# Sink keys once in K, and q's low half over all 128 rows

## The chip, the cores and the metric

One core of one Trainium2 chip. The metric is the device time of the program in microseconds (us), the median of several runs. A profiled execution is read beside it.

## The reference

Three layers in a row, all in float32. First attention with a window and sinks: 4 batches, 8 heads, 768 positions, head width 64. A position sees itself and the 127 before it, and the first 4 positions (the sinks) always.

```python
scores = scale * np.matmul(q, k.transpose(0, 1, 3, 2))
is_sink = pos[None, :] < int(n_sink)
in_window = (rel >= 0) & (rel < int(window))
scores = np.where(is_sink | in_window, scores, -1000000000.0)
a = np.exp(scores - np.max(scores, axis=-1, keepdims=True))
out = np.matmul(a / (np.sum(a, axis=-1, keepdims=True) + 1e-09), v)
```

The result, 3072 tokens of 512, goes through a dense layer, `g = h - tanh(h)` with `h = x @ w_in` (width 2048) and `g @ w_out`. Then each token is sent to one of 8 experts (width 1024, relu) by the largest of 8 logits, and the expert's output is weighted by the token's gate.

## The kernel before

The tokens are worked on in 12 chunks of 256. A chunk's attention is 8 units, one a head; a unit U is two query blocks t = 0, 1 of 128 positions. Each chunk then passes the dense layer in 16 steps of 128 hidden columns (`L1`, `gact`, `L2`), and `r_route` gives its tokens their places in the experts' pages. After the last chunk the pages of 256 tokens pass their experts (`m_L1`, `m_L2`).

float32 products are made from float32r operands split into a high half (a cast) and a low half (the value minus the cast): three products, high by high, high by low, low by high. For the scores of units from 14 on (`nf=14`; the first 14 take plain float32) the halves are stacked in the 128 rows, since the head width is 64. `a_split` (line 292) gets q and k with their 64 rows twice. ScalarE casts q to A over 128 rows (299). POOL overwrites A's rows 64 to 127 with q's low half (300, recorded at the helper's line 216). Two DMAs on the SP queue fill B with A's halves the other way round (301, 302). VectorE casts k to K (303) and overwrites K's lower rows with k's low half (304). `a_S` (307) multiplies A and then B by the same 288 columns of K (314, 315), into one PSUM tile s.

K's 448 columns are: the block before, 32 sink keys, block 0, the 32 sink keys again, block 1. Query block t takes the 288 columns from 160 t on: the block before it, the sinks, its own block. Own and earlier scores are merged by a predicated copy on VectorE (319), where the mask `mgt` is set for columns beyond the row, so that 128 columns hold the window. Then VectorE adds the mask and takes the row's extreme (326), ScalarE takes the exponential (328), POOL normalises (337), TensorE transposes (347, 348), POOL selects the two triangles (355), and TensorE multiplies by V (413 to 419), which ScalarE casts and POOL subtracts just as A is (288, 289; rows 128). In the dense layer POOL makes the low half of g with the same kind of subtraction (201, line 216 too), on 128 rows.

`r_route` ends, once a chunk, with two indirect DMAs on POOL's own queue that scatter the tokens' gates and numbers to their slots in DRAM (656). They come up on POOL between the subtractions.

The order: `run_chunks` gives every action a due time (unit U at 2 U - 15.64 steps, chunk c at 16 c, with offsets from the table of options in line 45), sorts by it, and emits. The framework then lays out each engine's queue by a simulated timeline of its own, so neighbours can change places (line 302's copy is issued ahead of line 301's), and puts in the semaphore waits. Each engine runs its own queue in order. Loads of q, k, v wait on the SP queue for one of two buffers (`raw=2`), A, B and K have two each (`sp=2`), V one. SP also issues the copies to B and the weights' loads.

Of the kernel before, what the change touches and what calls it, by code (L numbers as in the profile page):

```python
# [11 lines left out]
U8 = mybir.dt.uint8  # L12
AF = mybir.ActivationFunctionType
ALU = mybir.AluOpType
PSUM = bass.MemoryType.PSUM

P = 128
B, H, S, D = 4, 8, 768, 64
# [2 lines left out]
NCH = NT // CH  # L21
NF = DFF // P
SK = 32
KW = 2 * (P + SK) + P
QW = P + SK + P
NEG = -8.0e9
NE, FF = 8, 1024
# [9 lines left out]
def f32(ap):  # L37
    return ap.bitcast(F32)


class Kern:
# [9 lines left out]
    def consts(self, cp):  # L51
        nc = self.nc
        self.ident = cp.tile([P, P], F32, name="ident")
        make_identity(nc, self.ident)
        self.mgt = cp.tile([P, P], U8, name="mgt")
        nc.vector.memset(self.mgt, 1)
        nc.gpsimd.affine_select(out=self.mgt.bitcast(mybir.dt.int8), in_=self.mgt.bitcast(mybir.dt.int8),
                                pattern=[[1, P]], base=0, channel_multiplier=-1,
                                compare_op=ALU.is_gt, fill=0.0)

    def scalars(self, cp):

# [188 lines left out]
    def a_load(self, U):  # L251
# [3 lines left out]
        if U < self.o["nf"]:  # L255
            if U % 2:
                q = f32(self.spp.tile([P, CH], F32R, tag="A", name=f"q{U}"))
                k = f32(self.spp.tile([P, KW], F32R, tag="K", name=f"k{U}"))
            else:
                q = self.rawp.tile([P, CH], F32, tag="q", name=f"q{U}")  # L260
                k = self.rawp.tile([P, KW], F32, tag="k", name=f"k{U}")
            nc.sync.dma_start(q[:D], self.a["q"][b, h, j, :D])
# [4 lines left out]
        q = p.tile([P, CH], F32, tag="q", name=f"q{U}")  # L267
        k = p.tile([P, KW], F32, tag="k", name=f"k{U}")
        nc.sync.dma_start(q, self.a["q"][b, h, j])
# [22 lines left out]
    def a_split(self, U):  # L292
        nc = self.nc
        u, p = self.u[U], self.spp
        q, k = u.pop("q"), u.pop("k")
        A = p.tile([P, CH], F32R, tag="A", name=f"A{U}")
        Bt = p.tile([P, CH], F32R, tag="B", name=f"B{U}")
        K = p.tile([P, KW], F32R, tag="K", name=f"K{U}")
        self.cast(self.e("qhi", U < 16), A, q)
        self.sub(self.e("qlo", U < 16), A[D:], q[D:], f32(A[D:]))  # L300
        nc.sync.dma_start(f32(Bt[:D]), f32(A[D:]))
        nc.sync.dma_start(f32(Bt[D:]), f32(A[:D]))
        self.cast(self.e("khi", U < 16), K, k)
        self.sub(self.e("klo", U < 16), K[D:], k[D:], f32(K[D:]))
        u.update(A=A, B=Bt, K=K)

    def a_S(self, U, t):
        nc = self.nc
        u = self.u[U]
        i = 2 * ((U // H) % 3) + t  # L310
        s = self.ps("s", F32, f"s{U}_{t}")
        kt = u["K" if "K" in u else "k"][:, t * (P + SK):t * (P + SK) + QW]
        if "A" in u:
            nc.tensor.matmul(s[:, :QW], u["A"][:, t * P:(t + 1) * P], kt, start=True, stop=False)
            nc.tensor.matmul(s[:, :QW], u["B"][:, t * P:(t + 1) * P], kt, start=False, stop=True)
        else:
            nc.tensor.matmul(s[:, :QW], u["q"][:D, t * P:(t + 1) * P], kt[:D], start=True, stop=True)
        if i > 0:
            nc.vector.copy_predicated(s[:, P + SK:QW], self.mgt, s[:, :P])
        p = self.smp  # L320
        if t == 0:
            u["sm"] = p.tile([P, 2], F32, tag="sm", name=f"sm{U}")
            u["e"] = {}
        nm = p.tile([P, 1], F32, tag="nm", name=f"nm{U}_{t}")
        e = p.tile([P, SK + P], F32, tag="e", name=f"e{U}_{t}", bufs=self.o["be"])
        nc.vector.tensor_tensor_reduce(out=e, in0=s[:, P:QW], in1=self.mask[min(i, 2)], scale=-0.125,  # L326
                                       scalar=3.0e38, op0=ALU.add, op1=ALU.min, accum_out=nm)
        nc.scalar.activation(e, e, AF.Exp, bias=nm, scale=-1.0, accum_out=u["sm"][:, t:t + 1])  # L328
        u["e"][t] = e
        if t == 1:  # L330
            nc.gpsimd.tensor_scalar(out=u["sm"], in0=u["sm"], scalar1=1e-9, scalar2=1.0, op0=ALU.add, op1=ALU.mult)
            nc.vector.reciprocal(u["sm"], u["sm"])  # L332
# [92 lines left out]
    def general(self):  # L425
        tc, nc = self.tc, self.nc
        SH = S // 2
        with ExitStack() as st:
# [7 lines left out]
            for i in range(S // P):  # L436
# [6 lines left out]
                k = kp.tile([P, S], BF16, name=f"gkeep{i}")  # L443
                nc.vector.tensor_tensor(out=k, in0=inw, in1=sink, op=ALU.max)
                keep.append(k)
            for b in range(B):
                for h in range(H):
                    n = f"{b}_{h}"
                    q = lp.tile([D, S], F32, tag="q", name="gq" + n)
                    k = lp.tile([D, S], F32, tag="k", name="gkk" + n)  # L450
                    v = lp.tile([P, S // P, D], F32, tag="v", name="gv" + n)
                    for j in range(S // CH):
                        nc.sync.dma_start(q[:, j * CH:(j + 1) * CH], self.a["q"][b, h, j, :D])
                        for r in range(2):
                            o = P + SK + r * (P + SK)
                            nc.sync.dma_start(k[:, (2 * j + r) * P:(2 * j + r + 1) * P], self.a["k"][b, h, j, :D, o:o + P])
                        nc.sync.dma_start(v[:, 2 * j:2 * j + 2], self.a["v"][b, h, j, :, 1:3])
                    for i in range(S // P):
                        m = f"{n}_{i}"
                        s = wp.tile([P, S], F32, tag="s", name="gs" + m)  # L460
                        for z in range(2):
                            ps = pp.tile([P, 512], F32, tag="s", name=f"gps{m}_{z}")
                            nc.tensor.matmul(ps[:, :SH], q[:, i * P:(i + 1) * P], k[:, z * SH:(z + 1) * SH],
                                             start=True, stop=True)
                            nc.scalar.mul(s[:, z * SH:(z + 1) * SH], ps[:, :SH], 0.125)
                        t = wp.tile([P, S], F32, tag="t", name="gt" + m)
                        nc.vector.tensor_mul(s, s, keep[i])
                        nc.vector.tensor_scalar(out=t, in0=keep[i], scalar1=1.0e9, scalar2=-1.0e9, op0=ALU.mult, op1=ALU.add)
                        nc.vector.tensor_add(s, s, t)
                        nm = wp.tile([P, 1], F32, tag="nm", name="gnm" + m)  # L470
                        sm = wp.tile([P, 1], F32, tag="sm", name="gsm" + m)
                        nc.vector.tensor_reduce(out=nm, in_=s, axis=mybir.AxisListType.X, op=ALU.max, negate=True)
                        nc.scalar.activation(s, s, AF.Exp, bias=nm, accum_out=sm)
                        nc.vector.tensor_scalar(out=sm, in0=sm, scalar1=1e-9, scalar2=None, op0=ALU.add)
                        nc.vector.reciprocal(sm, sm)
                        nc.vector.tensor_scalar(out=s, in0=s, scalar1=sm, scalar2=None, op0=ALU.mult)
                        x = pp.tile([P, 512], F32, tag="x", name="gx" + m)
                        for z in range(S // P):
                            tp = pp.tile([P, 512], F32, tag="t", name=f"gtp{m}_{z}")
                            nc.tensor.transpose(tp[:, :P], s[:, z * P:(z + 1) * P], self.ident)  # L480
                            at = wp.tile([P, P], F32, tag="at", name=f"gat{m}_{z}")
                            nc.scalar.copy(at, tp[:, :P])
                            nc.tensor.matmul(x[:D, :P], v[:, z], at, start=(z == 0), stop=(z == S // P - 1))
                        xo = wp.tile([D, P], F32, tag="xo", name="gxo" + m)
                        nc.vector.tensor_copy(xo, x[:D, :P])
                        c = b * (S // CH) + i // 2
                        o = (h % 2) * D
                        nc.sync.dma_start(self.xd[c, h // 2, o:o + D, (i % 2) * P:(i % 2 + 1) * P], xo)
# [459 lines left out]
def layouts(inp):  # L948
    import numpy as np
    a = {}  # L950
    q, k, v = inp["q"], inp["k"], inp["v"]
# [3 lines left out]
    sk = kT[..., :SK]  # L955
    blk = [kT[..., i * P:(i + 1) * P] for i in range(6)]
    hs = []
    for j in range(3):
        b0 = 2 * j
        one = np.concatenate([blk[max(b0 - 1, 0)], sk, blk[b0], sk, blk[b0 + 1]], axis=3)  # L960
        hs.append(np.concatenate([one, one], axis=2))
    a["k"] = np.ascontiguousarray(np.stack(hs, axis=2))
    vb = [v[:, :, i * P:(i + 1) * P] for i in range(6)]
# [3 lines left out]
    for j in range(3):  # L967
        b0 = 2 * j
# [35 lines left out]
```

## Time and profile before

| | us |
|---|---|
| median of 3 runs (1222.67 to 1223.86) | 1222.8 |
| the profiled execution | 1225.8 |
| its span, first to last instruction | 1224.0 |
| TensorE matmuls busy | 1135.9 (93%) |
| VectorE busy | 885.5 (72%) |
| ScalarE busy | 757.4 (62%) |
| POOL busy | 657.7 (54%) |
| mean granted TensorE clock, share of 2.4 GHz | 0.96 |

The engines' names in the profile are PE (TensorE; PEld its weight loads), DVE (VectorE), ACT (ScalarE), POOL (GpSimd) and SPq (the SP queue, which only issues DMAs). Attention and the dense layer take the first 850 us or so, the experts the rest. An engine's idle time costs something only where TensorE, the busiest, waits for it in the end. Tiles carry the program's names, with buffer numbers left out.

### The profile page before, as it was taken

How to read it: one execution, taken by the hardware profiler on the slowest of the kernel's cores; microseconds unless marked ns; L12 is line 12 of the kernel's file. 1: busy time of each engine (PE TensorE's matmuls, PEld its weight loads, DVE VectorE, ACT ScalarE, POOL GpSimd, SP SyncE). 2: the span in 40 equal slices, each digit the busy share in tenths (PEclk: the TensorE clock that was granted, in tenths of full speed). 3: DMA queues.
4: the chain of work that ended last, by engine and by line, in shares of the span. 5: the costliest groups of instructions: out<-in, count | busy, mean ns of one | idle time of the engine just before them, and what ended most of it. 6: DMA issues, size and time to landing. Idle time of an engine off the chain costs nothing. (4 is left out here: it accounts for less than half of the span.)

```text
span 1224.0 us, 23714 instructions
## 1 busy us (share of the span) xinstructions
PE 1135.9 (93%) x7171; PEld 994.8 (81%) x7171; DVE 885.5 (72%) x2419; ACT 757.4 (62%) x2123; POOL 657.7 (54%) x973
## 2 busy tenths in 40 slices
PE   7879998999899899999899999999798999999993
PEld 3447787988789789989789988988687989999992
DVE  6889896888778687978778887966647566666720
ACT  3445765777577678767577877775726555555620
POOL 4987865777667668767667767763302211211200
PEclk9859998999999899999999999999998999999997
DMA  7654232333323233333333323200909777777500
GB/s 206 203 187 137 75 91 62 102 80 102 60 76 90 71 88 85 98 69 104 60 91 83 104 66 87 81 12 19 343 19 327 238 226 213 222 241 219 168 26 6
DMA packets 88256, 147.98 MB, mean 121 GB/s; under 512 B 18864, under 2 KB 64432, under 8 KB 88112
## 3 DMA queue, kind: packets, MB, share of 16 engines
q1 hardware_dynamic: 83184, 133.16, 37.2%
q0 software_dynamic: 4928, 13.14, 3.0%
q8 instruction: 61, 1.00, 0.4%
q14 instruction: 83, 0.68, 0.2%
HBM read 122.86 MB, written 13.17 MB: 111 GB/s over the span
## 5 line engine op out<-in xcount | busy, mean ns | idle before, releaser
L172 PE MATMUL h<-xt,wi 128*128 128x256 f32 x2304 | 356.1, 290 | 9.9 <-DVE gz L188 9.0
L246 PE MATMUL acc<-wo,g 128*128 128x512 f32 x1152 | 334.5, 407 | 24.0 <-POOL g L216 23.1
L172 PEld LDWEIGHTS h<-xt,wi 128*128 128x128 f32 x2304 | 320.5, 194 | 40.4 <-DVE gz L188 12.4
L246 PEld LDWEIGHTS acc<-wo,g 128*128 128x128 f32 x1152 | 198.6, 192 | 53.1 <-POOL g L216 26.0
L216 POOL TENSOR_TENSOR g<-gz,g 128x256 fp32r<-128x256 f32 x192 | 153.4, 802 | 82.3 <-ACT g L211 78.4
L735 DVE TENSOR_TENSOR ml<-mr,mh 128x1024 fp32r<-128x1024 f32 x104 | 127.9, 1236 | 53.4 <-ACT mh L734 51.8
L778 PE MATMUL mh<-mxt,mh 128*128 128x256 f32 x832 | 157.9, 286 | 3.2 <-DVE mxt L768 2.5
L795 PE MATMUL macc<-mh,mg 128*128 128x512 f32 x416 | 147.9, 401 | 4.3 <-DVE mg L782 4.3
L778 PEld LDWEIGHTS mh<-mxt,mh 128*128 128x128 f32 x832 | 138.1, 193 | 12.1 <-DVE mxt L768 2.9
L189 ACT ACTIVATE u<-u,kt 128x256 f32<-128x256 f32 x192 | 97.8, 509 | 80.2 <-DVE gz L188 73.8
L355 POOL TENSOR_SCALAR_AFFINE_SELECT X<-fl 128x512 fp32r<-128x512 f32 (+1 forms) x192 | 119.2, 643 | 33.6 <-DVE fl L385 24.5
L804 POOL DMA_INDIRECT out_dram<-mo,mi x26 | 28.5, 1096 | 200.2 <-ACT mo L803 196.0
L734 ACT CAST mh<-mr 128x1024 fp32r<-128x1024 f32 x104 | 108.6, 1052 | 40.9 <-PE macc L795 25.2
L188 DVE TENSOR_TENSOR gz<-u,h 128x256 f32<-128x256 f32 x192 | 78.9, 414 | 57.5 <-POOL g L216 34.2
L778 PE MATMUL mh<-mxt,ml 128*128 128x256 f32 x416 | 118.5, 286 | 0.0
L194 DVE SCALAR_TENSOR_TENSOR gz<-gy,gz 128x256 f32<-128x256 f32 x192 | 108.3, 570 | 9.2 <-ACT gy L185 2.7
L328 ACT ACTIVATE e<-e,nm 128x160 f32<-128x160 f32 x192 | 82.0, 427 | 48.0 <-DVE nm L326 46.5
L211 ACT CAST g<-gz 128x256 fp32r<-128x256 f32 x192 | 77.0, 402 | 44.4 <-DVE gz L194 29.7
L337 POOL TENSOR_SCALAR e<-e,sm 128x160 f32<-128x160 f32 x192 | 96.9, 515 | 11.6 <-DVE sm L332 9.6
L216 POOL TENSOR_TENSOR A<-q,A 64x256 fp32r<-64x256 f32 x82 | 69.4, 846 | 56.3 <-issue 14.0
L781 ACT ACTIVATE mg<-mh 128x256 fp32r<-128x256 f32 x104 | 40.3, 387 | 94.2 <-PE mh L778 88.3
L185 ACT ACTIVATE gy<-u,k 128x256 f32<-128x256 f32 x192 | 96.5, 510 | 2.5
(211 smaller groups left out, 2270.5 us busy)
## 6 DMA issues: line engine op xcount, KB each, us to landing
mr<-in_moe_w_dram SPq DMA_DIRECT2D x104, 512.0 KB, 4.7
k<-in_k_dram SPq DMA_DIRECT2D x82, 224.0 KB, 2.7
v<-in_v_dram SPq DMA_DIRECT2D x96, 128.0 KB, 2.3
q<-in_q_dram SPq DMA_DIRECT2D x82, 128.0 KB, 2.2
B<-A SPq DMA_DIRECT2D x164, 64.0 KB, 2.1
rawi<-in_moe_w_in_dram SPq DMA_DIRECT2D x16, 512.0 KB, 5.7
rawo<-in_moe_w_out_dram SPq DMA_DIRECT2D x16, 512.0 KB, 5.6
x2d<-x SPq DMA_DIRECT2D x24, 256.0 KB, 2.2
```

The source lines that it names most:

```text
L172: nc.tensor.matmul(h[:, :CH], w[:, wl, k * P:(k + 1) * P], x[:, xl, k], start=(n == 0), stop=(n == 11))
L185: nc.scalar.activation(y, u, AF.Square, bias=self.k0, scale=K1)
L189: nc.scalar.activation(u, u, AF.Relu, bias=self.kt, accum_out=self.over[:, n:n + 1])
L194: nc.vector.scalar_tensor_tensor(out=z, in0=y, scalar=KC, in1=z, op0=ALU.add, op1=ALU.mult)
L216: (self.nc.vector if eng == "v" else self.nc.gpsimd).tensor_tensor(out=out, in0=a, in1=b, op=ALU.subtract)
L246: nc.tensor.matmul(o, g[:, gl, t * P:(t + 1) * P], w[:, wl], start=(f == 0 and n == 0), stop=(f == NF - 1 and n == 2))
L337: self.nc.gpsimd.tensor_scalar(out=e, in0=e, scalar1=r, scalar2=1.0, op0=ALU.mult, op1=ALU.mult)
L355: self.nc.gpsimd.affine_select(out=out, in_=in_, pattern=[[0, n], [s, P]], base=0, channel_multiplier=-s, compare_op=ALU.is_gt if prev els ...
L734: nc.scalar.copy(hi, r)
L735: nc.vector.tensor_sub(lo, r, f32(hi))
L778: nc.tensor.matmul(h, w[:, k * P:(k + 1) * P], x[:, xl, k], start=(n == 0), stop=(n == 11))
L795: nc.tensor.matmul(self.macc[g][t], gt[:, gl, t * P:(t + 1) * P], w[:, DM:], start=(f == 0 and n == 0), stop=(f == n8 - 1 and n == 2))
```

## The change

K keeps the sink keys once, in 416 columns: the block before, the sinks, block 0, block 1. Query block 0 takes columns 0 to 287 as before. Block 1 takes columns 128 to 415, which are the sinks, block 0, block 1; its own scores are copied over those of its neighbour where a second mask, `mge`, is set (row not less than column), and the 160 columns from the front are used. B is no longer filled by two DMAs from A: A stays q's high half in all 128 rows, and POOL writes q's low half to all 128 rows of B in one subtraction. With K's high half above and its low half below, A and B times K give the same four products as before.

```diff
-KW = 2 * (P + SK) + P
+KW = 3 * P + SK
...
-        nc.gpsimd.affine_select(out=self.mgt.bitcast(mybir.dt.int8), in_=self.mgt.bitcast(mybir.dt.int8),
-                                pattern=[[1, P]], base=0, channel_multiplier=-1,
-                                compare_op=ALU.is_gt, fill=0.0)
+        self.mge = cp.tile([P, P], U8, name="mge")
+        nc.vector.memset(self.mge, 1)
+        for m, s, op in ((self.mgt, 1, ALU.is_gt), (self.mge, -1, ALU.is_ge)):
+            m = m.bitcast(mybir.dt.int8)
+            nc.gpsimd.affine_select(out=m, in_=m, pattern=[[s, P]], base=0, channel_multiplier=-s,
+                                    compare_op=op, fill=0.0)
...
         self.cast(self.e("qhi", U < 16), A, q)
-        self.sub(self.e("qlo", U < 16), A[D:], q[D:], f32(A[D:]))
-        nc.sync.dma_start(f32(Bt[:D]), f32(A[D:]))
-        nc.sync.dma_start(f32(Bt[D:]), f32(A[:D]))
+        self.sub(self.e("qlo", U < 16), Bt, q, f32(A))
...
-        kt = u["K" if "K" in u else "k"][:, t * (P + SK):t * (P + SK) + QW]
+        kt = u["K" if "K" in u else "k"][:, t * P:t * P + QW]
...
-        if i > 0:
+
+        if t:
+            nc.vector.copy_predicated(s[:, SK:P + SK], self.mge, s[:, P + SK:QW])
+        elif i > 0:
             nc.vector.copy_predicated(s[:, P + SK:QW], self.mgt, s[:, :P])
+        s = s[:, :P + SK] if t else s[:, P:QW]
...
-        nc.vector.tensor_tensor_reduce(out=e, in0=s[:, P:QW], in1=self.mask[min(i, 2)], scale=-0.125,
+        nc.vector.tensor_tensor_reduce(out=e, in0=s, in1=self.mask[min(i, 2)], scale=-0.125,
...
-        one = np.concatenate([blk[max(b0 - 1, 0)], sk, blk[b0], sk, blk[b0 + 1]], axis=3)
+        one = np.concatenate([blk[max(b0 - 1, 0)], sk, blk[b0], blk[b0 + 1]], axis=3)
```

`general`, which runs only where the inputs don't fit the fast path, takes its columns of k from the new places.

## Rows read from the trace of the kernel before

**Rows 1.** The page, part 1: busy time, share of the span, instructions.

```profile
PE 1135.9 (93%) x7171; PEld 994.8 (81%) x7171; DVE 885.5 (72%) x2419; ACT 757.4 (62%) x2123; POOL 657.7 (54%) x973
```

**Rows 2.** Stretches: length, busy (instructions) of PE, PEld, DVE, ACT, POOL, PEclk, DMA share, GB/s.

```profile
395.83:468.56 72.73, 67.45 (x448) 61.35 (x447) 54.13 (x171) 49.76 (x162) 47.42 (x77) 0.95 0.33 81
468.56:529.31 60.75, 60.47 (x423) 55.67 (x422) 52.10 (x170) 46.42 (x153) 46.56 (x74) 1.00 0.32 87
...
667.20:728.01 60.81, 60.50 (x423) 55.70 (x422) 52.09 (x170) 46.43 (x153) 46.63 (x74) 1.00 0.32 87
```

**Rows 3.** TensorE's waits from 190 to 802 us: total us, times, longest.

```profile
PE acc L246 <- POOL g L216: 22.4, 8, 5.6
PE R L413 <- POOL V L216: 4.6, 2, 2.3
PE T L347 <- POOL e L337: 1.5, 5, 0.5
```

**Rows 4.** TensorE in order of time: start, us, what [idle before, releaser].

```profile
266.02 1.19 PE L246 MATMUL acc<-wo,g 128*128 128x512 f32 x4 [0.75 <-POOL g L216]
...
405.96 1.22 PE L246 MATMUL acc<-wo,g 128*128 128x512 f32 x2 [4.51 <-POOL g L216]
```

**Rows 5.** POOL in order of time around 400 us.

```profile
395.83 0.97 POOL L656 DMA_INDIRECT xs<-pl,sl  x1 [0.30 <-issue]
396.82 0.75 POOL L216 TENSOR_TENSOR g<-gz,g 128x256 fp32r<-128x256 f32 x1
403.70 0.72 POOL L216 TENSOR_TENSOR A<-q,A 64x256 fp32r<-64x256 f32 x1 [6.13 <-issue]
```

**Rows 6.** DMA issues from 395.7 to 396.6 us: KB, us to landing.

```profile
k<-in_k_dram SPq DMA_DIRECT2D x1, 224.0 KB, 6.2
xs<-pl,sl POOLq DMA_INDIRECT x1, 7.6
```

**Rows 7.** POOL in order of time around 470 us.

```profile
468.56 0.97 POOL L656 DMA_INDIRECT xs<-pl,sl  x1 [0.30 <-DMA B<-A]
...
470.29 0.74 POOL L216 TENSOR_TENSOR V<-v,V 128x256 fp32r<-128x256 f32 x1
...
475.50 0.74 POOL L216 TENSOR_TENSOR A<-q,A 64x256 fp32r<-64x256 f32 x1
```

**Rows 8.** Groups by line and form: busy us, mean ns | idle before, releasers.

```profile
L216 POOL TENSOR_TENSOR A<-q,A 64x256 fp32r<-64x256 f32 x82 | 69.4, 846 | 56.3 <-issue 14.0 <-DMA k<-in_k_dram 12.2 <-ACT A L211 9.2
L216 DVE TENSOR_TENSOR K<-k,K 64x448 fp32r<-64x448 f32 x82 | 68.1, 830 | 2.6
L216 POOL TENSOR_TENSOR V<-v,V 128x256 fp32r<-128x256 f32 x82 | 62.9, 767 | 29.5 <-ACT V L211 25.2 <-PE T L348 1.9 <-DMA B<-A 0.2
...
L213 DVE CAST K<-k 128x448 fp32r<-128x448 f32 x82 | 43.8, 534 | 0.0
```

**Rows 9.** ScalarE in order of time: the cast for the g behind V.

```profile
399.37 0.39 ACT L211 CAST g<-gz 128x256 fp32r<-128x256 f32 x1
```

**Rows 10.** Stretches right behind stalls, columns as in rows 2.

```profile
201.75:207.00 5.25, 5.25 (x19) 4.86 (x20) 3.92 (x10) 3.23 (x11) 4.56 (x9) 0.50 0.16 49
...
736.50:739.50 3.00, 3.00 (x12) 2.81 (x13) 2.42 (x8) 1.59 (x6) 2.90 (x6) 0.51 0.28 78
801.13:805.00 3.87, 3.87 (x25) 3.50 (x26) 2.94 (x9) 2.50 (x9) 3.17 (x7) 1.00 0.14 38
```

**Rows 11.** The page, part 6: DMA issues, KB each, us to landing.

```profile
k<-in_k_dram SPq DMA_DIRECT2D x82, 224.0 KB, 2.7
...
B<-A SPq DMA_DIRECT2D x164, 64.0 KB, 2.1
```

**Rows 12.** The SP queue's own waits: total us, times, longest.

```profile
SPq L302 <- PE s L315: 213.8, 71, 5.3
```

**Rows 13.** TensorE in order of time: the unit whose A was made at 403.70.

```profile
416.01 0.30 PE L314 MATMUL s<-K,A 128*128 128x288 f32 x1
```

**Rows 14.** The start: POOL in order of time.

```profile
9.62 0.19 POOL L331 TENSOR_SCALAR sm<-sm 128x2 f32<-128x2 f32 x1 [5.49 <-ACT e L328]
```

More of the change, by code (lines that the diff above doesn't have):

```diff
@@ L454, in general @@
                         for r in range(2):
-                            o = P + SK + r * (P + SK)
+                            o = P + SK + r * P
                             nc.sync.dma_start(k[:, (2 * j + r) * P:(2 * j + r + 1) * P], self.a["k"][b, h, j, :D, o:o + P])
```

## The prediction, made before the changed kernel was run

> **What bounds the kernel now.** Read the page first: TensorE is busy for 93% of the span [rows 1], so time can only be won where it waits or where its clock is low. Then the stretches by chunk: from one chunk's last scatter of slots (line 656) to the next. The stretch from 468.56 us has TensorE at work for 60.47 of 60.75 us at full clock; the one before it takes 72.73 us with 67.45 us of work at a mean clock of 0.95 [rows 2]. Both hold a chunk's work (448 matmuls against 423). So there is no slow engine to look for, but something that happens at some chunk borders and not at others. Third, TensorE's waits from 190 to 802 us: 22.4 us for POOL's g (line 216) in 8 waits, 4.6 us for POOL's V in 2 [rows 3]; everything else there is below 1.6 us a row. One of the 8 is the 0.75 us at 266.02, the typical large one the 4.51 us before 405.96 [rows 4].
>
> Fourth, POOL around the large one. The second scatter ends at 396.80, a 128-row subtraction (g) starts at 396.82, and then POOL stands for 6.13 us until the subtraction that makes q's low half, A<-q,A, 64 rows, at 403.70 [rows 5]; V and g follow it. The profile names nothing for that wait ("issue"), and another name at other borders. What fits is the landing of the scatter: issued at 395.83, it lands 7.6 us later, at 403.43 [rows 6]. At eight of the ten borders from 190 to 802 us A starts 0.3 to 0.6 us after the second landing; this is the fourth of them. At the two where the plan puts A late, here at 475.50, POOL works from 468.56 on, V (128 rows, the same operation) goes at 470.29, and TensorE loses nothing [rows 7, 2]. So the border's wait belongs to the 64-row subtraction alone: it does not start before everything that POOL issued earlier, the scatter's transfer included, is done. 128-row subtractions never stand so.
>
> **The change part by part.**
>
> 1. *q's low half over 128 rows into B.* The 64-row A<-q,A (846 ns, 82 times) becomes one 128-row B<-q,A. The nearest row is V<-v,V at 767 ns; were the price by rows it would be twice 846 [rows 8]. I take 767, for g and V with 128 rows are no slower than A with 64: 82 x 0.08 = 6 us less of POOL, off the path. What counts is the wait. By the V and g rows a 128-row subtraction is not held for the scatter, so the seven stalls go: 22.4 + 4.6 - 0.75 = 26.2 us [rows 3, 4]. At the sample border the new order would be scatter to 396.80, g to 397.57, B, V, and the next g when ScalarE's cast has ended at 399.76 [rows 9], done by 400.5; TensorE stood from 405.96 - 4.51 = 401.45. The slack is about 1 us, so the stall goes wholly, but not by much.
>
> 2. *The clock.* Behind six of the seven stalls the granted clock is at the lower level (1.2 GHz): 5.25 us at 0.50 after the stall that ends at 201.75, 3.00 us at 0.51 after the one that ends at 736.50, and none after the 1.37 us stall that ends at 801.13 [rows 10]. TensorE was busy all through these stretches, with 19 matmuls in 5.25 us where 25 fit in 3.87 us at full clock, so half of each is lost: 2.6, 2.8, 2.9, 1.7, 1.7 and 1.5 us, 13.2 us in six (first and last are shown). With no idleness ahead of them they stay at 2.4 GHz, as at the border of 468.56 [rows 2].
>
> 3. *Both copies B<-A go.* 164 issues on the SP queue (64 KB each as the page counts, 2.1 us to landing) vanish [rows 11], and with them the queue's head-of-line wait: the SP queue stood 213.8 us before line 302, in 71 waits for the last readers of B [rows 12]. That wait now stands on POOL, in front of B<-q,A; queued behind it are V, g and the normalising of e, and TensorE waits for those. But B<-q,A needs the new A, whose cast already waits for the score matmuls of the same unit two back, as A has two buffers like B. So B's wait ends at most one matmul later (0.30 us [rows 13]), or at once; I take nothing. Loads of q, k and v behind those issues start earlier, and hold buffers that are free anyway: nothing. First score matmul of the unit whose A was made at 403.70: 416.01 [rows 5, 13], 11.6 us after the subtraction's end; the copy's 2.1 us was hidden in that and is worth nothing.
>
> 4. *K with 416 columns.* Cast 534 ns and low half 830 ns on VectorE [rows 8], both at most 7% less: 82 x 0.097 = 8 us of VectorE, at least nothing. VectorE is at 52.10 of 60.75 us where TensorE is at 60.47 [rows 2], so this is hidden under TensorE; uncovered it would be a gain. The k load is 7% smaller; TensorE's first matmul waits for one, and 7% of its 2.7 us [rows 11] is 0.2 us, which I leave out of the sum.
>
> 5. *The merge.* The second block copies its own scores over its neighbour's where before it did the reverse: same count, same 128x128 predicated copy, same 128x160 reduction, same 288 moving columns. Nothing. The second mask adds one select on POOL at the start, which fits into the 5.49 us that POOL idles there before its first sums [rows 14], and one memset on VectorE. Nothing.
>
> **Sum.** The profiled execution took 1225.8 us, 3.0 above the median of the runs, 1222.8. Minus 26.2, minus 13.2, plus what a border at which POOL doesn't stand still shows (0.75 us at the one before 266.02 [rows 4], none at 468.56 and 667.20, where TensorE is at work for all but 0.3 us of the stretch [rows 2]; mean 0.25, times seven: 1.8): 1188.2 us. Carried to the median: 1185.2. I say 1185.
>
> **A rule that speaks against it.** POOL's row: g with 128 rows starts 0.02 us after the scatter's instruction ends [rows 5]. The Trainium skill, "GPSIMD Engine Reference", sections 1 and 4, says that each of POOL's eight cores owns 16 partitions and that a pair of them writes the descriptors of POOL's DMAs; "DMA: Bandwidth & Descriptors", on software and hardware descriptor generation, names cores 0 and 1. By that the old subtraction on the upper 64 rows had no share in those cores, and the new one would have to stand behind the descriptors. The sum by the row is as above; a full stand behind two scatter instructions of 0.97 us at each of seven borders would take 14 us back, if none of it were hidden. The trace speaks for the row.
>
> **The rivals.**
>
> *B. The stalls shrink, but something else at the border holds POOL or TensorE.* For it: the slack of 1 us is thin, a k load caught by the scatter takes 6.2 us instead of 2.7 [rows 6, 11], and the order on every queue is laid anew by the build. Against: loads have a unit's time, some 8 us, to spare, and the borders at 468.56 and 667.20 pass without loss. If half of the gain stays: 1222.8 - 20 = 1203.
>
> *C. The wait isn't the 64 rows'; any subtraction on a freshly loaded q is held for the scatter.* Then B stands where A stood, and the change does not do what counts. For it: all waits seen are those of this one line. Against: V is also made from a fresh load and passes the scatter. Time: 1222.8 less 0.2 for the first load, so 1222.
>
> *D. Slower: score matmuls move ahead of POOL.* Without the copies the build may place the score matmuls, and the wait for B, nearer to the subtraction, and TensorE, which runs its queue in order, stands at line 315 for POOL. Against: the distance is 11.6 us now [rows 5, 13]. It decides when the mean wait in 82 units passes 39.4 / 82 = 0.48 us; at 0.6 us the kernel takes 1222.8 + 10 = 1233.
>
> **How the numbers follow.** Forecast 0.80, B 0.12, C 0.05, D 0.03. What a measurement of this kernel can tell from no change is about 0.2%, 2.4 us. The forecast alone reaches from 1173 (TensorE's other waits of 190 to 802 us, some 4 us, and POOL's and VectorE's relief come on top) to 1196 (two borders remain, or the new order costs 10 us). The range goes on to B: 1173 to 1206. Faster 0.92 (forecast and B), same 0.05 (C), slower 0.03 (D).
>
> **What would show it.** Right: no B<-A on the SP queue; B<-q,A with 128 rows at about 770 ns; POOL going on within 0.3 us of each scatter; TensorE's wait for g and V from 190 to 802 us below 4 us instead of 27.0; full clock from 105 to 880 us; chunk stretches of 60 to 65 us. Wrong: a wait of several us in front of B<-q,A behind a scatter (C), a new row "PE s L315" for POOL (D), low clock without a stall ahead of it, or a start before 190 us that is laid out anew by more than 5 us.

## The result and the profile after

| | before | after |
|---|---|---|
| median of the runs, us | 1223.3 (4 runs, 1222.7 to 1224.7) | 1185.6 (4 runs, 1184.6 to 1186.0) |
| ratio, 95% interval | | 0.969 [0.967, 0.971] |
| span of the profiled execution, us | 1224.0 | 1183.6 |
| TensorE busy, us | 1135.9 | 1125.5 |
| TensorE idle in the span, us | 88.1 | 58.1 |

The kernel is 38 us faster; the forecast was 1185. The span fell by 40.4 us: TensorE idles 30.0 us less, and the same 7171 matmuls keep it busy for 10.4 us less, which is the clock (worked out by stage below). By stage, cut at the second scatter of the first and of the last chunk, the start went from 192.3 to 189.5 us, the middle from 721.0 to 683.4, and the end stayed at 310.8 and 310.6. So the gain lies where the forecast put it.

The page of the changed kernel: part 1 (compare [rows 1]) and the packets.

```profile
PE 1125.5 (95%) x7171; PEld 986.2 (83%) x7171; DVE 878.2 (74%) x2420; ACT 757.5 (64%) x2123; POOL 655.9 (55%) x974
...
DMA packets 75133, 135.74 MB, mean 115 GB/s; under 512 B 16240, under 2 KB 51312, under 8 KB 74992
```

TensorE's waits in the changed kernel from 189 to 802 us (total us, times, longest), against [rows 3]. The lines are those of the changed file: 246 is now 249, 413 is 418, 216 is 219.

```profile
PE h L175 <- DVE gz L191: 2.0, 3, 0.9
...
PE R L418 <- POOL V L219: 0.6, 2, 0.5
...
PE acc L249 <- POOL g L219: 0.3, 1, 0.3
```

The 27.0 us of waits for g and V are 0.9. POOL at two chunk borders of the changed kernel, in order of time, against [rows 5]:

```profile
316.19 1.19 POOL L661 DMA_INDIRECT xs<-pl,sl  x1 [0.30 <-issue]
317.38 0.78 POOL L219 TENSOR_TENSOR g<-gz,g 128x256 fp32r<-128x256 f32 x1
318.07 0.77 POOL L219 TENSOR_TENSOR B<-q,A 128x256 fp32r<-128x256 f32 x1
318.77 0.76 POOL L219 TENSOR_TENSOR g<-gz,g 128x256 fp32r<-128x256 f32 x1
319.48 0.97 POOL L219 TENSOR_TENSOR V<-v,V 128x256 fp32r<-128x256 f32 x1
...
632.46 0.99 POOL L661 DMA_INDIRECT xs<-pl,sl  x1 [0.31 <-PE T L353]
633.47 0.76 POOL L219 TENSOR_TENSOR B<-q,A 128x256 fp32r<-128x256 f32 x1
```

This is the order that the forecast wrote down for its sample border, with no gap, but that V and the second g have changed places. At 632.46 B even follows the scatter directly, 0.02 us after its end. At all ten borders from 189 to 762 us POOL goes on within 0.1 us of the scatter's end. Some chunk stretches of the changed kernel (columns as in [rows 2]):

```profile
256.05:316.19 60.14, 58.68 (x402) 52.97 (x401) 50.15 (x167) 44.23 (x144) 43.96 (x71) 1.00 0.24 67
...
442.48:507.72 65.24, 63.06 (x431) 57.18 (x431) 53.06 (x173) 48.81 (x157) 46.78 (x75) 1.00 0.25 69
...
632.46:700.60 68.14, 67.29 (x464) 61.45 (x462) 56.17 (x181) 51.93 (x170) 48.93 (x77) 1.00 0.30 70
```

All nine stretches from 189.53 to 760.34 run at full clock, and TensorE is busy for 562.24 of 570.81 us. They are not equal, because the scatter's place in the order moves, and with it the number of matmuls between two scatters (402 to 464); read the busy share, not the length. What is left on POOL and on SP, by groups and by waits (the SP queue's rows against [rows 12]):

```profile
L219 POOL TENSOR_TENSOR B<-q,A 128x256 fp32r<-128x256 f32 x82 | 69.6, 849 | 17.3 <-ACT A L214 16.4 <-PE h L175 0.4
L219 POOL TENSOR_TENSOR V<-v,V 128x256 fp32r<-128x256 f32 x82 | 63.9, 780 | 26.3 <-ACT V L214 25.7
```

```profile
SPq L272 <- POOL B L219: 196.6, 64, 6.9
SPq L273 <- DVE K L219: 155.2, 42, 9.1
```

POOL's idle time in front of this subtraction fell from 56.3 us [rows 8] to 17.3, nearly all of it for ScalarE's cast. The SP queue's long wait did not go away: it moved from the copy to the next load of q.

### The profile page after: what moved, and what is told of

The parts are those of the page before. It is cut to its first block, busy times and chain, and to the rows that moved or that the text cites. A ratio compares the mean times of both kernels' runs of the same rounds, so it can differ in the third digit from the quotient of the medians.

```text
span 1183.6 us, 23222 instructions
## 1 busy us (share of the span) xinstructions
PE 1125.5 (95%) x7171; PEld 986.2 (83%) x7171; DVE 878.2 (74%) x2420; ACT 757.5 (64%) x2123; POOL 655.9 (55%) x974
## 5 line engine op out<-in xcount | busy, mean ns | idle before, releaser
L175 PE MATMUL h<-xt,wi 128*128 128x256 f32 x2304 | 351.3, 290 | 7.9 <-DVE gz L191 6.8
L249 PE MATMUL acc<-wo,g 128*128 128x512 f32 x1152 | 330.4, 402 | 4.7 <-POOL g L219 2.7
L249 PEld LDWEIGHTS acc<-wo,g 128*128 128x128 f32 x1152 | 195.3, 189 | 32.0 <-POOL g L219 4.4
L342 POOL TENSOR_SCALAR e<-e,sm 128x160 f32<-128x160 f32 x192 | 95.8, 509 | 12.6 <-DVE sm L337 10.4
L800 PEld LDWEIGHTS macc<-mh,mg 128*128 128x128 f32 x416 | 77.8, 190 | 17.3 <-DVE mg L787 4.5
```

The costliest lines, as they stand in the source:

```text
L175: nc.tensor.matmul(h[:, :CH], w[:, wl, k * P:(k + 1) * P], x[:, xl, k], start=(n == 0), stop=(n == 11))
L249: nc.tensor.matmul(o, g[:, gl, t * P:(t + 1) * P], w[:, wl], start=(f == 0 and n == 0), stop=(f == NF - 1 and n == 2))
L342: self.nc.gpsimd.tensor_scalar(out=e, in0=e, scalar1=r, scalar2=1.0, op0=ALU.mult, op1=ALU.mult)
L800: nc.tensor.matmul(self.macc[g][t], gt[:, gl, t * P:(t + 1) * P], w[:, DM:], start=(f == 0 and n == 0), stop=(f == n8 - 1 and n == 2))
```

## The experiments

They ran in three series on three chips, on which the kernel before took 1214.0, 1215.1 and 1214.2 us. The first has q's part alone, the keys' part alone and the first pair of small instructions; the second the changed kernel once more, the halves exchanged, the copies kept and q's low half on VectorE; the third the kernel before for its trace, the second pair and the version with V's low half on VectorE too. Each ratio is against the kernel before in the same series; between the series the kernel before differs by up to 1.1 us.

### Which part of the change

**q's part alone**, on the kernel before:

```diff
-        self.sub(self.e("qlo", U < 16), A[D:], q[D:], f32(A[D:]))
-        nc.sync.dma_start(f32(Bt[:D]), f32(A[D:]))
-        nc.sync.dma_start(f32(Bt[D:]), f32(A[:D]))
+        self.sub(self.e("qlo", U < 16), Bt, q, f32(A))
```

> The kernel before with only q's part of the change: q's low half is subtracted over 128 rows straight into B and both copies of A's halves go; the keys stay at 448 columns and the merge stays as it was. Theory (the gain is POOL's hold behind the scatters): all of the gain but at most 1 us, 1184 to 1188 us; GpSimd goes on within 0.3 us of each scatter and the chunk stretches are 60 to 68 us. Rival 1 (the shorter keys and the merge on the other side make the gain): 1218 to 1224 us. Rival 2 (part each, through VectorE's 8 us): 1192 to 1200 us.

Measured: 1185.35 us, ratio 0.976 [0.973, 0.979]. TensorE's wait for g from 190 to 765 us is 0.3 us. As far as these runs can tell, all of the gain is in this part.

**The keys' part alone** (the changed kernel with the lines above turned back):

> The changed kernel with q's part undone: the low half is again 64 rows of A on GpSimd, and both copies into B are back; the keys stand in 416 columns and odd query blocks merge to their neighbour's side, as in the change. Theory: the stalls behind the scatters are all there, PE waits for g and V some 25 us, and the time is within 3 us of the kernel before, 1219 to 1224 us. Rival 1 (keys and merge make the gain): 1184 to 1188 us.

Measured: 1204.43 us, ratio 0.992 [0.989, 0.995]. Neither expectation holds: the keys and the merge alone bring 10 us. POOL at one border, and TensorE's wait for g from 189 to 788 us (17.1 us in the trace of the kernel before in the third series, below):

```profile
390.64 0.97 POOL L663 DMA_INDIRECT xs<-pl,sl  x1 [0.30 <-issue]
391.68 0.74 POOL L219 TENSOR_TENSOR g<-gz,g 128x256 fp32r<-128x256 f32 x1
392.37 0.74 POOL L219 TENSOR_TENSOR V<-v,V 128x256 fp32r<-128x256 f32 x1
393.20 0.19 POOL L338 TENSOR_SCALAR sm<-sm 128x2 f32<-128x2 f32 x1
393.46 1.47 POOL L362 TENSOR_SCALAR_AFFINE_SELECT X<-fl 128x512 fp32r<-128x512 f32 x2
```

```profile
PE acc L249 <- POOL g L219: 13.3, 5, 4.1
```

Shorter instructions on K give the framework other times for its own timeline, and it lays every queue in another order. At this border, as at [rows 7], V and selects stand between the scatter and the 64-row subtraction, and the scatter's rows land meanwhile. At others (189.79, 321.90, 644.79 us) POOL still stands. TensorE's waits for g and V are 14.5 us here against 18.0 in that trace, and it is busy for 1129.2 us against 1131.7: 6.0 of the 7.3 us between the two traces. So most of it is a smaller dose of the same thing; that the rest is too was not shown. The next run asks whether there is a second gain.

**The changed kernel itself, in the second series:**

> The changed kernel once more, beside the runs of this chip, where the kernel before took 1214 us and the kernel with q's part alone 1185. If the keys' part adds nothing on top of q's part: 1182 to 1188 us. If its 10 us with the copies still there (1204 against 1214) are another gain than q's: 1174 to 1178 us.

Measured: 1184.08 us, ratio 0.975 [0.972, 0.977], against 0.976 [0.973, 0.979] for q's part alone in the first series. On top of q's part, the keys' part adds nothing that these runs can tell.

### What holds the subtraction

The forecast said: a subtraction on 64 rows is held. In the changed kernel the rows, the place, the copies and the tile are all different at once. The sharpest test leaves everything and exchanges the halves in A: the low half goes to rows 0 to 63. B then holds them the other way round, and the same four products come out.

```diff
-        self.sub(self.e("qlo", U < 16), A[D:], q[D:], f32(A[D:]))
+        self.sub(self.e("qlo", U < 16), A[:D], q[:D], f32(A[:D]))
```

> The kernel before with q's two halves exchanged in A: GpSimd subtracts the low half into rows 0 to 63 and the high half stays in rows 64 to 127; both copies into B, the sub's 64 rows and the order of every queue are as before. Theory (only an instruction that starts at row 64 is held behind the scatters): the stalls go and the time is that of q's part alone, 1182 to 1190 us. Rival 1 (any 64-row instruction is held, as the forecast said): 1210 to 1224 us. Rival 2 (the copies, their traffic or their waits on the SP queue, made the stalls): 1205 to 1224 us.

To set beside it, the kernel before was profiled in the third series:

> The kernel before, profiled beside the other runs, to set it against the kernel with the halves exchanged, whose queues hold the same instructions in the same order. Theory: GpSimd does nothing from the end of a scatter, or of the one instruction behind it, until 0.1 us after its rows have landed, at 7 of 10 borders, and TensorE's waits for g and V there are 20 to 30 us in all; a time of 1210 to 1224 us, and half-clock stretches behind most of the stalls. If the time is near 1214 us with the same stalls, what the chips differ in is the clock behind them.

Measured: 1186.13 us with the halves exchanged, ratio 0.976 [0.974, 0.979]; 1212.17 us in the one run of the kernel before. Every engine has the same instructions in the same order in both built programs. POOL at the same border, first the kernel before, then with the halves exchanged:

```profile
390.73 0.97 POOL L656 DMA_INDIRECT xs<-pl,sl  x1 [0.31 <-issue]
391.70 0.77 POOL L216 TENSOR_TENSOR g<-gz,g 128x256 fp32r<-128x256 f32 x1
397.32 0.72 POOL L216 TENSOR_TENSOR A<-q,A 64x256 fp32r<-64x256 f32 x1 [4.85 <-PE s L315]
```

```profile
381.71 0.97 POOL L656 DMA_INDIRECT xs<-pl,sl  x1 [0.30 <-issue]
382.70 0.76 POOL L216 TENSOR_TENSOR g<-gz,g 128x256 fp32r<-128x256 f32 x1
383.40 0.75 POOL L216 TENSOR_TENSOR A<-q,A 64x256 fp32r<-64x256 f32 x1
384.10 0.74 POOL L216 TENSOR_TENSOR V<-v,V 128x256 fp32r<-128x256 f32 x1
```

TensorE's waits for POOL's g and V from 190 to 790 us in the kernel before here, and for g from 190 to 770 us with the halves exchanged (which has no row for V):

```profile
PE acc L246 <- POOL g L216: 17.1, 8, 5.0
...
PE R L413 <- POOL V L216: 0.9, 1, 0.9
```

```profile
PE acc L246 <- POOL g L216: 0.3, 1, 0.3
```

The kernel before waits for 18.0 us here, less than the 20 to 30 that were expected, and its time is within the range. With the halves exchanged the scatter of 381.71 lands 6.7 us after its issue, at 388.4, and A starts at 383.40, long before.

So not the 64 rows, and not the copies, but that the instruction starts at row 64. The built programs show what stands in front of it. These are the same four places of POOL's queue, behind the first chunk's scatters, with the waits that the framework put in: the kernel before, then with the halves exchanged.

```
L656 DMA xs<-pl,sl [waits DVE]
L656 DMA xs<-pl,sl
L216 TENSOR_TENSOR A<-q,A 64x256 [waits DMAHW0,DMASW1,DMAHW1,DMASW0,DMAHW3,Activation,Pool]
L216 TENSOR_TENSOR V<-v,V 128x4x64 [waits PE,DMAHW4,Activation,Pool]

L656 DMA xs<-pl,sl [waits DVE]
L656 DMA xs<-pl,sl
L216 TENSOR_TENSOR A<-q,A 64x256 [waits DMAHW1,DMAHW3,DMAHW0,Activation]
L216 TENSOR_TENSOR V<-v,V 128x4x64 [waits DMAHW4,PE,Activation]
```

DMASW0 and DMASW1 are the two scatters' landings, Pool is POOL's own earlier work. With rows 64 to 127 the subtraction waits for both, and V, behind it, for the subtraction; with rows 0 to 63 those waits are not there. In the whole program all 82 subtractions from row 64 wait for POOL's own earlier work and 10 of them for a scatter; of the 82 from row 0 none waits for either.

**An instruction that does nothing else.** If this is the whole cause, any small instruction from row 64 on brings the stalls back. To the changed kernel a subtraction of 2 columns was added in each split, into a scratch tile that nothing reads:

```diff
+        self.scr = cp.tile([P, 2], F32, name="scr")
...
         self.sub(self.e("qlo", U < 16), Bt, q, f32(A))
+        self.sub("g", self.scr[D:], q[D:, :2], q[D:, :2])
```

> The changed kernel, and in each split one more GpSimd subtraction of 2 columns on rows 64 to 127, from q into a scratch tile that nothing reads. Its own time is small, 82 times perhaps 0.1 to 0.3 us off the path. Theory (what held GpSimd was not the sub's size or its data but that it starts at row 64): the holds behind the scatters return, PE waits for g and V over 15 us, half-clock stretches behind the stalls, 1203 to 1226 us. Rival (the hold came from the copies, from the sub's place or from what reads A): 1184 to 1190 us.

and with `[:D]` for `[D:]`:

> The same extra subtraction of 2 columns, but on rows 0 to 63. Theory in its narrow form (rows from 64 on are held, rows from 0 on are not): 1184 to 1190 us, no hold behind the scatters. In its wide form (any instruction on fewer than 128 rows is held, as the forecast put it): 1203 to 1226 us, as with the upper rows.

Measured: 1234.1 us (ratio 1.016 [1.013, 1.018]) on the upper rows and 1213.5 us (0.999 [0.998, 1.001]) on the lower. The two have the same queues, so 20.6 us come from the rows alone. But both lie above their ranges: the upper one above 1226, and the lower one should have been near 1185. POOL's waits of the lower one (total us, times, longest) say why:

```profile
POOL scr L220 <- DMA q<-in_q_dram: 64.7, 48, 3.1
```

The little instruction needs nothing but the load of q, so the framework put it early in POOL's queue, and there it stands for the load with POOL's real work behind it. This was a fault of the experiment. The pair was run again with `f32(Bt[D:, :2])` in q's place, which POOL has just written:

> The extra subtraction of 2 columns again, on rows 64 to 127 of the changed kernel, now from B, which GpSimd has just written, so that it waits for no load. Theory: held behind the scatters as before, 1195 to 1215 us, 10 to 25 us more than on rows 0 to 63. Rival (the 20.6 us between the first pair came through the wait for q's load): within 3 us of the run on rows 0 to 63.

> The same extra subtraction from B on rows 0 to 63. If the first pair's 1213 us came from GpSimd's waits for q's load ahead of its own work (48 waits, 64.7 us): 1184 to 1192 us, its own 82 times 0.19 us being off the path. If 82 more instructions on GpSimd are dear in themselves, or the order that the framework makes of them is: 1200 to 1215 us.

Measured: 1208.67 us (0.995 [0.993, 0.997]) on the upper rows, 1194.56 us (0.984 [0.982, 0.986]) on the lower; again the queues are the same, and the rows alone make 14.1 us, inside the 10 to 25 that were expected. In this pair both instructions read what POOL has just written, so in both built programs all 82 wait for POOL's own work; what differs is the wait for a scatter, which 9 of the upper 82 have and none of the lower. POOL at the same border, upper rows, then lower:

```profile
325.19 0.98 POOL L663 DMA_INDIRECT xs<-pl,sl  x1 [0.30 <-issue]
329.25 0.19 POOL L220 TENSOR_TENSOR scr<-B 64x2 f32<-64x2 f32 x1 [3.08 <-DMA xs<-pl,sl]
329.53 0.19 POOL L338 TENSOR_SCALAR sm<-sm 128x2 f32<-128x2 f32 x1
```

```profile
319.48 0.98 POOL L663 DMA_INDIRECT xs<-pl,sl  x1 [0.30 <-PE s L318]
320.47 0.21 POOL L220 TENSOR_TENSOR scr<-B 64x2 f32<-64x2 f32 x1
320.77 0.19 POOL L338 TENSOR_SCALAR sm<-sm 128x2 f32<-128x2 f32 x1
```

Here the profile names the releaser outright: the scatter's landing. An instruction of 0.19 us holds POOL for 3.08 us. The lower run, 10 us above the changed kernel, falls between its two expectations (to 1192, and from 1200): with the waits for q's load gone, 18.9 of the first pair's 29.4 us above the changed kernel are gone, not all. Whether the 82 instructions or the new order that they cause (TensorE's queue differs in some 3600 of its places) cost the rest was not taken apart.

### The copies, and a version that is faster still

**The copies kept**, with the subtraction on 128 rows:

```diff
-        self.sub(self.e("qlo", U < 16), Bt, q, f32(A))
+        L = p.tile([P, CH], F32R, tag="L", name=f"L{U}")
+        self.sub(self.e("qlo", U < 16), L, q, f32(A))
+        nc.sync.dma_start(f32(Bt[:D]), f32(L[:D]))
+        nc.sync.dma_start(f32(Bt[D:]), f32(L[D:]))
```

> The changed kernel, but the 128-row subtraction writes a tile L, and two DMAs of 64 rows each copy L into B on the SP queue, where the copies stood before. Theory (the copies' 164 issues cost nothing): 1182 to 1189 us. Rival (the copies delay the loads behind them on the SP queue, or the scores by the 2.1 us until they land): 1190 to 1215 us.

Measured: 1185.53 us, ratio 0.976 [0.974, 0.978], against the changed kernel's 1184.08. TensorE's queue is the same, and 164 DMAs with 2.3 us each to landing cost at most 1.5 us.

**q's low half on VectorE:**

```diff
-        self.sub(self.e("qlo", U < 16), Bt, q, f32(A))
+        self.sub("v", Bt, q, f32(A))
```

> The changed kernel with q's low half made by VectorE in place of GpSimd. GpSimd loses 82 times 0.85 us, VectorE gains 82 times some 0.4 to 0.6 us. If GpSimd's load is still what makes TensorE wait between the borders: 1174 to 1182 us. If TensorE is the bound at 95% busy and VectorE has room: 1182 to 1188 us. If VectorE becomes late with the dense layer's products: 1190 to 1210 us.

**and V's as well** (`vlo='v'`):

> The changed kernel with the low halves of both q and V made by VectorE. GpSimd loses 82 more subtractions of 0.78 us, VectorE gains 82 of some 0.45 us and comes to 79% busy. If less on GpSimd still pays, as moving q's did (1184 to 1178 us): 1170 to 1177 us. If VectorE is now the later one: 1180 to 1195 us.

Measured: 1178.44 us (ratio 0.971 [0.968, 0.973]) and 1179.01 us (0.971 [0.968, 0.973]). The first is faster than the changed kernel: its four runs are 1178.05 to 1180.10, the changed kernel's 1182.82 to 1184.89. The second lies between its two ranges and is no faster than the first. The group by line of VectorE's new subtraction in the first, and the stretch from the first chunk's second scatter to the tenth's (columns as in [rows 2]); then the same stretch of the changed kernel in the second series:

```profile
L219 DVE TENSOR_TENSOR B<-q,A 128x256 fp32r<-128x256 f32 x82 | 40.1, 489 | 0.5
```

```profile
193.50:760.50 567.00, 562.62 (x3897) 514.87 (x3896) 490.60 (x1616) 432.17 (x1399) 361.98 (x596) 1.00 0.25 70
```

```profile
190.50:760.60 570.10, 562.18 (x3876) 513.06 (x3875) 474.34 (x1540) 429.77 (x1392) 415.84 (x665) 1.00 0.25 69
```

VectorE makes it in 489 ns where POOL needs 849. TensorE is busy for 99.2% of the stretch instead of 98.6%, and 21 more matmuls fall into it. Moving V's too changed nothing more that these runs can tell. That the first gain is POOL's load and not the order of the queues, which moves here as well, was not shown.

## Why the prediction was right, step by step

**The wait (part 1): right, its size nearly, its rule too wide.** 26.2 us were to go; TensorE's waits for g and V went from 27.0 to 0.9. "The border's wait belongs to the 64-row subtraction alone" is true of this kernel, and the reason in the same step, that it waits for all that POOL issued before, is what the built program says. But 64 rows are not the condition: 64 rows from row 0 pass (1186.13 us). The traces of the kernel before had no POOL instruction of 64 rows from row 0 to tell the two apart. The change removes the condition in either case, so the number came out.

**The price of B: mis-sized.** I took V's 767 ns; it took 849, as the 64-row subtraction did with 846 [rows 8]. In these traces POOL's subtraction for q costs the same on 64 rows as on 128, and more than V's (780 ns on 128 rows). The 6 us of relief did not come; they lay off the path.

**The clock (part 2): the cause right, 13.2 us a little too much.** TensorE's busy time fell by 10.4 us. The difference is in two stretches of the changed kernel at half clock that the forecast did not have (columns as in [rows 2]):

```profile
122.39:125.81 3.42, 3.42 (x16) 3.27 (x16) 3.02 (x8) 3.39 (x11) 2.60 (x3) 0.50 0.39 137
828.95:832.37 3.42, 3.42 (x18) 3.33 (x17) 3.35 (x6) 1.34 (x4) 0.81 (x1) 0.50 1.04 383
```

By the forecast's own working, half of each is lost, 3.4 us together, and 13.2 less 3.4 is 9.8. By stage it fits as well: the busy time fell by 11.3 us in the middle (682.4 to 671.0), where the second stretch lies, and rose by 1.2 in the start (169.6 to 170.8), where the first lies. Both stand behind a wait of TensorE: 1.85 us for gz before 122.23, and 2.28 us for g before 828.46. The second has no held subtraction behind it. POOL, in order of time:

```profile
824.36 1.74 POOL L758 DMA_INDIRECT mx<-x2d,ms  x1 [4.20 <-DVE ms L752]
826.40 0.96 POOL L758 DMA_INDIRECT mx<-x2d,ms  x1 [0.31 <-issue]
827.38 1.02 POOL L219 TENSOR_TENSOR g<-gz,g 128x256 fp32r<-128x256 f32 x1
```

The experts' first gathers stand in POOL's queue for their indices, and the last chunk's g behind them. In the two traces whose queues do not differ at all, from the second and third series, the halves exchanged take 15.9 us of TensorE's idle time (78.6 to 62.7 us) and 8.8 of its busy time (1131.7 to 1122.9). So about a third of the gain is clock there (8.8 of 24.7 us of span), and a quarter in the first pair (10.4 of 40.4).

**The copies (part 3): nothing, as forecast.** With them kept, the kernel takes 1185.5 us, and in the kernel with the halves exchanged they are there untouched at 1186.1. But the SP queue's wait did not come to stand on POOL, as the forecast had it: it is 196.6 us before the next load of q, and B waits 16.4 us for A's cast and 0.4 for TensorE.

**K (part 4): nothing in the end, but by a way that the forecast left out.** The cast takes 526 ns for 534 and the low half 789 for 830, 82 x 0.049 = 4 us of VectorE, hidden. The forecast priced these edits by their own durations only. On the kernel before, K and the merge are worth 10 us: the queues are laid anew, and fewer held subtractions stand right behind a scatter, which accounts for most of it. With the hold gone, that has nothing to act on.

**The merge (part 5): nothing.** It ran only together with K; the two add nothing to q's part.

**The rivals.** B (half of the stalls stay) falls: of the 27.0 us of waits for g and V 0.9 are left, and the one larger wait for g has another cause. C (any subtraction on a fresh q is held) falls with the rows of 632.46. D: the changed kernel has no row for a wait of line 316 on POOL. The rule that spoke against the change, that a 128-row instruction stands behind the descriptors of the scatter, would show as time between the end of the scatter and B: it is 0.02 us at 632.46, and in the kernel with the halves exchanged A starts at 195.06, as the scatter of 194.08 ends. By the rows there is no such stand here.

**The signs.** Three did not hold: full clock from 105 to 880 us (the two stretches above), chunk stretches of 60 to 65 us (59.7 to 68.1, since they hold unequal work), and B at about 770 ns (849). In rival C, 1222.8 less 0.2 rounds to 1223, not 1222.

**The number: closer than its working.** In the middle TensorE's idle time fell by 26.2 us (38.6 to 12.4) where the sum had 24.4 (26.2 less 1.8), and its busy time by 11.3 where it had 13.2; the two misses cancel, 37.5 against 37.6. The start, which the forecast left alone, became 2.7 us shorter, so the profiled executions lie 40.4 us apart and not 37.6. That the medians still meet the forecast comes from the execution that was profiled before: it took 3.0 us more than the median, and the one after 0.3 less than its own. So the mechanism was right, and a hit within 1 us was luck.

## What to carry to other kernels

Look at the first row of every POOL instruction, not only at its size: here one that starts at row 64 is fenced by the build against all of POOL's earlier work, DMA landings included, and where one came up behind a scatter, POOL stood for 3 to 7 us. Putting the half that POOL writes into rows 0 to 63, or writing all 128, cost nothing here. When a build lays the queues anew, compare kernels whose queues are the same before believing any 1%; an added instruction of 0.2 us can cost far more by the wait that it brings to the place that it is given.

## What the runs showed of the hardware that was not expected

The subtraction on POOL takes as long on 64 rows as on 128: 846 ns and 849 ns in the mean (850 ns on rows 0 to 63).

The wait from row 64 on is in the built program. The Trainium skill, "GPSIMD Engine Reference", section 2.1, says that POOL's cores, each with 16 rows, do not wait for one another between instructions, and asks for a wait on the producer's semaphore where one reads what another wrote. The waits printed above are waits on such semaphores, but in this kernel nothing that the subtraction into A reads was written by POOL or by the scatters. No run here shows why rows from 64 on get them and rows from 0 on do not.

The start can run at half clock for 41 us and lose little. These are the same 40.9 us of the start, first with the halves exchanged (second series), then in the kernel before (third series), with the same queues:

```profile
55.10:96.00 40.90, 33.52 (x92) 19.55 (x93) 36.09 (x68) 17.71 (x53) 33.81 (x37) 0.50 0.48 155
```

```profile
55.10:96.00 40.90, 33.06 (x115) 20.07 (x114) 36.81 (x74) 19.52 (x58) 35.58 (x37) 0.96 0.54 176
```

The first reaches its first chunk border at 194.1 us, the second at 191.0, so 40 us at half clock cost some 3 us, unless the chips or the halves make a part of that: VectorE and POOL are busy for 34 to 37 of the 41 us, and TensorE has room. Among the runs of the kernel with the halves exchanged, the two with a mean clock of 0.97 took 1187.2 us and the two at 0.99 took 1184.9. A half-clock stretch in the middle, where TensorE is busy throughout, costs half of its length [rows 10].

The kernel before took 1223 us where the first pair ran and 1214 to 1215 beside the experiments; the changed one 1185.6 and 1184.1. Most of the difference is the stall: of 13.7 us between the two traces of the kernel before, TensorE's waits for g and V make 9.0 (27.0 and 18.0 us), and its busy time 4.2. Why the stalls are shorter in one was not taken apart. So the change is worth 38 us in the first pair and some 30 us in the series behind it.
